# Packing the next key tile's scores into the void half of a causal diagonal block

## The chip, the cores and the metric

The kernel runs on one core of one Trainium2 chip, as one launch. The metric is the time of a run on the device in microseconds (us), lower is better. Engines are called as in the profile: PE is TensorE's matmul side, PEld its weight loads, ACT is ScalarE, DVE is VectorE, POOL is GpSimd, SP is SyncE, which issues the DMAs.

## The reference

The layer has 2048 tokens of width 576 and 32 heads of width 18, cut into 4 segments of 512 tokens. Weights and activations are bfloat16. Inside a segment attention is causal; between segments a compressive memory is read and updated. A feed-forward network of width 4608 follows.

```
for s in range(4):                         # segments of L = 512 tokens
    qs, ks, vs = q[:, :, s], k[:, :, s], v[:, :, s]        # (32 heads, 512, 18)
    p = softmax(qs @ ks.T * 18**-0.5 + causal_mask)        # exp of 512 x 512 scores for each head
    a_dot = p @ vs
    a_mem = (phi(qs) @ M) / (phi(qs) @ z + 1e-6)           # memory; phi(t) = t+1 if t>0 else exp(t)
    out_s = g * a_mem + (1 - g) * a_dot
    M += phi(ks).T @ vs;  z += phi(ks).sum(rows)
h  = x + concat(out) @ wo                  # q, k, v come from layernorm(x) @ (wq, wk, wv)
h2 = h + gelu(layernorm(h) @ w1 + b1) @ w2 + b2
```

## The kernel before

**Heads and tiles.** Four heads make a group g (8 groups). A group's transposed queries and keys lie in four bands of 32 partitions, one head in each. A score matmul takes one band: 32 rows of the array, 128 keys as weights, up to 512 queries as the moving side. Four of them, one for each band, run beside each other and write four banks of PSUM; the profile shows each as `32*128`. The value product works the other way: 128 keys are the rows, 19 columns (18 of the head and a one that sums the denominator) are the weights, four heads lie beside each other in bands of 32 columns. The profile shows it as `128*19`.

**Scores of segments 1 to 3** (`stage_A`, L1105). For 128 keys `kt` only the queries from `kt*128` on are needed, so the four key tiles of a group have 512, 384, 256 and 128 columns. Two groups (a pair) fill five steps of 512 columns by the table `STEPS` (L951), whose entries are (group of the pair, key tile, first column, width). A step is one score operation (`st`, L1163), one exp of all 4 x 512 columns on ACT (`exp`, L1167) and a mask for each diagonal block of 128 x 128 (`mask`: a product with the triangle `tri` on DVE, L1176, or a select on POOL, L1178). Half of each diagonal block is void: keys that lie behind the query. Then the group's value product (`val`, L1189) reads four such pieces, `valT` (L1197) transposes it, `rec2`, `comb` and `comb2` scale it and add the memory's part (`mem`, L1134 or L1137, `memT`, `memfin`). Per segment there are 20 steps, 8 `val` and 32 masks.

**Scores of segment 0** (`stage_A0`, L970) are made in smaller portions as soon as tokens are there: 20 steps in parts A00 to A03 (`st0`, L1002; exp L1005). Six of them hold four diagonal blocks of 128 columns each (16 matmuls); the others hold off-diagonal or wide pieces.

**The exp's results** go to five buffers `pt` of 128 x 4 x 512. A score step takes four of the eight PSUM banks.

**The rest of PE's work.** Projections (`Pk`, `Pq`, `Pv`, L835, 64 rows), the output projection (`Po`, `Ro`, L793, or L819 where both lie next to each other and are done with 128 rows), transposes (L738, L881), memory sums (`M`, L928), the network's first product (`F1`, L1301 and L1338, 64 rows) and its second (`F2`, L1388, 128 rows).

**The order** is a table written by a planner outside the kernel. `TIMETABLE` (L25) gives each operation its rank and its engine, `schedule` (L396) emits all operations by rank, and each engine then runs its own list strictly in that order. Semaphores between the engines follow from which tiles are read and written, in the order of emission. The cost figures in `add(...)` serve the planner and the choice of buffers only.

**The start.** DVE fills a part of the first `pt` buffer with zeros (`warm_ok`, L638); PE runs eight matmuls on it (`warm`, L644) until the first layernorm is there, then transposes it (`TX`, L738). POOL builds the identity matrix, the triangle, and fills padding.

Of the kernel before, what the change touches and what calls it, by code (L numbers as in the profile page):

```python
# [12 lines left out]
ALU = mybir.AluOpType  # L13
# [12 lines left out]
    "A00exp": "a 75 88",  # L26
    "A00mask": "g 93 111 177 101",
    "A00st0": "p 69 87",
    "A01comb": "d156 g187 g201 g210",
    "A01exp": "a 125 141 165 152",  # L30
    "A01mask": "g127 g126 d168 g181",
    "A01oT": "d 179 191 229 218 231",
    "A01rec": "d 153 159 195 207",
    "A01st0": "p 124 140 164 147",
    "A01swap": "d225 g230",
    "A01val": "p 150 184",
    "A01valT": "d 151 157 192 206",
    "A02comb": "g 318 352",
    "A02exp": "a 204 222 214 247 259 277 291",
    "A02mask": "g261 g242 g260 d320",  # L40
    "A02rec": "d 287 342",
    "A02st0": "p 198 221 213 237 252 270 290",
    "A02val": "p 274 278 307 324",
    "A02valT": "d 279 326",
    "A03comb": "g 416 446",
    "A03exp": "a 312 344 329 351 363 370 385",
    "A03mask": "g358 g345 g357 d392",
    "A03oT": "d 362 360 418 447 459",
    "A03rec": "d 378 432",
    "A03st0": "p 308 330 327 348 359 369 384",  # L50
    "A03swap": "g 448 453",
    "A03val": "p 367 372 421 422",
    "A03valT": "d 376 426",
    "A0flip": "s 110 84 113 118 160 175 284 298",
    "A1comb": "g535 d581 d630 g676 d708 g737 g773 d783",
    "A1comb2": "g549 g604 g634 g689 g719 d758 d779 d785",
    "A1eg": "a 393 430 520 593 584 653 617 714",
    "A1exp": "a 395 450 429 523 516 538 562 570 607 586 627 666 637 680 703 694 733 741 749 718",
    "A1flip": "s 383 424 470 509 488 606 583 678",
    "A1mask": "d456 g466 g515 g495 g474 g547 g537 g545 g620 g585 d572 d602 g645 g633 g643 d616 g661 d681 g672 g674 d705 d686 d712 g713 d744 g757 g756 g762 "  # L60
        "d755 d766 g730 g735",
    "A1mem": "p 442 513 578 649 613 722 691 745",
    "A1memT": "d 443 514 579 655 622 726 692 761",
    "A1memfin": "g499 d590 g611 g657 d659 d752 g747 d784",
    "A1oT": "d 673 732 798 809 810",
    "A1pq": "d 407 458 536 639 601 699 667 736",
    "A1rec": "d 462 565 589 656 652 740 697 770",
    "A1rec2": "d 521 573 625 660 698 725 772 782",
    "A1rg": "g 406 454 497 619 559 651 631 721",
    "A1st": "p 394 444 425 522 503 528 561 569 598 580 626 663 636 679 702 693 729 734 748 715",  # L70
    "A1swap": "g806 d793",
    "A1val": "p 518 568 623 646 695 723 763 780",
    "A1valT": "d 519 571 624 658 696 724 764 781",
    "A2comb": "g889 d921 d968 d997 g1029 g1063 g1127 g1148",
    "A2comb2": "g904 g922 g973 d1013 d1047 g1079 g1133 g1149",
    "A2eg": "a 751 727 872 924 984 939 1008 1052",
    "A2exp": "a 796 774 804 790 816 906 919 871 934 945 963 989 1001 979 1011 1028 1046 1078 1069 1092",
    "A2flip": "s 706 668 818 843 819 888 967 1037",
    "A2mask": "d805 d803 g788 d822 g849 d885 g855 d861 d923 g959 d937 g957 g892 g964 d954 g965 g981 d991 d992 g1016 d1025 d1032 g1042 d1014 d1070 d1090 "
        "g1050 g1098 g1085 g1096 g1128 g1104",  # L80
    "A2mem": "p 835 859 911 938 1019 971 1059 1101",
    "A2memT": "d 836 866 913 956 1024 975 1060 1102",
# [1467 lines left out]
```

## Time and profile before

| | |
|---|---|
| runs | 447.46, 448.99, 449.4 us; median 448.99 |
| profiled execution | span 444.7 us from the first to the last instruction; its own total is not given, so 4.3 us lie between the span and the median |
| PE | busy 431.7 us, 97% of the span, 5355 matmuls |
| ACT | busy 296.7 us, 67% |
| DVE | busy 291.2 us, 65% |
| POOL | busy 179.3 us, 40% |
| granted TensorE clock | 0.999 |

Times are from one profiled execution; shares are of its span. A busy share says how long an engine had an instruction in flight. PE's matmuls are pipelined, so one may start while the one before it is still counted as busy; what an operation takes from PE is read from the distance between starts. A row of the timeline gives start, length, engine, line, operation, the tiles it writes and reads, the active rows and columns of the array, the operand's shape and how many instructions it merges. A row of the waits gives the engine and line that waited, what ended the wait, the total in us, the number of times and the longest.

### The profile page before, as it was taken

How to read it: one execution, taken by the hardware profiler on the slowest of the kernel's cores; microseconds unless marked ns; L12 is line 12 of the kernel's file. 1: busy time of each engine (PE TensorE's matmuls, PEld its weight loads, DVE VectorE, ACT ScalarE, POOL GpSimd, SP SyncE). 2: the span in 40 equal slices, each digit the busy share in tenths (PEclk: the TensorE clock that was granted, in tenths of full speed). 3: DMA queues.
4: the chain of work that ended last, by engine and by line, in shares of the span. 5: the costliest groups of instructions: out<-in, count | busy, mean ns of one | idle time of the engine just before them, and what ended most of it. 6: DMA issues, size and time to landing. Idle time of an engine off the chain costs nothing.

```text
span 444.7 us, 12623 instructions
## 1 busy us (share of the span) xinstructions
PE 431.7 (97%) x5355; PEld 278.3 (63%) x5355; DVE 291.2 (65%) x636; ACT 296.7 (67%) x269; POOL 179.3 (40%) x312
## 2 busy tenths in 40 slices
PE   8888999998999999999999999999999999999997
PEld 5666677765676776664445766654457775446775
DVE  5889888999899988867777987837765121010011
ACT  5999999999878798686798966752684002556000
POOL 5776756457748435734236559440011000000010
PEclk9999999999999999999999999999999999999999
DMA  6779989999999945693863355805463461550030
GB/s 208 204 250 246 271 264 279 228 228 244 236 257 348 315 152 166 175 242 69 245 190 52 107 146 161 201 2 153 131 210 111 101 171 39 169 194 1 1 107 28
DMA packets 85274, 76.73 MB, mean 173 GB/s; under 512 B 62945, under 2 KB 72545, under 8 KB 85217
## 3 DMA queue, kind: packets, MB, share of 16 engines
q1 hardware_dynamic: 85072, 75.83, 63.3%
q8 instruction: 42, 0.69, 0.7%
q10 hardware_dynamic: 144, 0.09, 0.1%
q14 instruction: 16, 0.12, 0.1%
HBM read 42.08 MB, written 18.87 MB: 137 GB/s over the span
## 4 chain that ended last, share of the span: by engine, by line
PE 75%; DVE 7%; DMA 6%; ACT 6%; POOL 2%; issue 2%; SPq 1%; POOLq 0%; DVEq 0%; ACTq 0%
PE bank L1388 27%; PE bank L1301 21%; PE bank L835 9%; PE bank L1338 6%; DMA w1g<-in_B_w_dram 4%; PE bank L1163 3%; ACT hT L1355 3%; PE bank L1189 3%; PE bank L793 2%; DMA x<-in_A_x_dram 2%; ACT pt L1167 1%; PE bank L1002 1%; PE bank L819 1%; DVE ln L710 1%; POOL pt L1178 1%
## 5 line engine op out<-in xcount | busy, mean ns | idle before, releaser
L1167 ACT ACTIVATE pt<-bank 128x2048 bf16<-128x2048 f32 x60 | 112.7, 1878 | 30.4 <-PE bank L1163 25.1
L1388 PEld LDWEIGHTS <-hT 128*128 128x128 bf16 x1152 | 110.2, 98 | 34.5 <-issue 7.0
L1301 PE MATMUL bank<-xreg,w1g 64*128 64x512 bf16 x972 | 108.0, 376 | 0.2 <-DMA w1g<-in_B_w_dram 0.2
L1301 PEld LDWEIGHTS <-w1g 64*128 64x128 bf16 x972 | 46.2, 94 | 57.1 <-issue 2.3
L1388 PE MATMUL bank<-w,hT 128*128 128x288 bf16 x576 | 78.3, 286 | 0.0
L1388 PE MATMUL bank<-w_lo,hT 128*128 128x288 bf16 x576 | 78.0, 286 | 0.0
L835 PE MATMUL bank<-hT,xreg 64*128 64x288 bf16 x864 | 58.0, 283 | 1.1 <-DVE qk_pad L634 0.6
L1306 ACT ACTIVATE hT<-bank,b_col 128x512 bf16<-128x512 f32 x36 | 22.5, 689 | 46.0 <-PE bank L1301 46.0
L1178 POOL TENSOR_SCALAR_AFFINE_SELECT pt<-pt 128x512 bf16<-128x512 bf16 x58 | 42.0, 737 | 27.1 <-ACT pt L1167 26.9
L835 PEld LDWEIGHTS <-xreg 64*128 64x128 bf16 x864 | 41.6, 94 | 14.3 <-issue 5.0
L1400 DVE TENSOR_TENSOR ot<-bank,hc 128x288 bf16<-128x288 f32 x32 | 13.8, 448 | 52.2 <-PE bank L1388 51.1
L1316 DVE TENSOR_SCALAR hT<-bank,b_col 128x512 bf16<-128x512 f32 x49 | 34.9, 742 | 18.6 <-PE bank L1301 18.5
L1374 POOL TENSOR_TENSOR hc<-hc,b_bc 128x576 f32<-128x576 f32 x9 | 11.7, 1297 | 82.0 <-DMA hc<-hd 82.0
L1005 ACT ACTIVATE pt<-bank 128x2048 bf16<-128x2048 f32 x20 | 37.6, 1880 | 2.8 <-PE bank L1002 2.1
L1338 PE MATMUL bank<-xreg,w1g 64*128 64x256 bf16 x648 | 38.3, 269 | 0.6 <-DMA w1g<-in_B_w_dram 0.6
L1338 PEld LDWEIGHTS <-w1g 64*128 64x128 bf16 x648 | 31.3, 94 | 6.4 <-issue 2.7
L1374 DVE TENSOR_TENSOR hc<-hc,b_bc 128x576 f32<-128x576 f32 x7 | 5.6, 817 | 43.8 <-DMA hc<-hd 43.8
L1321 ACT ACTIVATE hT<-hT 128x8192 bf16<-128x8192 bf16 (+2 forms) x6 | 31.8, 5321 | 1.7 <-DVE hT L1316 1.6
L1314 ACT ACTIVATE hT<-bank,b_col 128x512 bf16<-128x512 f32 x23 | 15.1, 685 | 21.9 <-PE bank L1301 21.6
L1176 DVE TENSOR_TENSOR pt<-pt,tri 128x512 bf16<-128x512 bf16 x38 | 21.5, 569 | 4.7 <-ACT pt L1167 4.7
L1163 PE MATMUL bank<-qk 32*128 32x512 bf16 (+3 forms) x384 | 23.8, 300 | 0.2
L1349 DVE TENSOR_TENSOR hT<-bank,b_col 128x512 bf16<-128x512 f32 x32 | 21.0, 681 | 3.8 <-PE bank L1338 3.4
(117 smaller groups left out, 564.1 us busy)
## 6 DMA issues: line engine op xcount, KB each, us to landing
w1g<-in_B_w_dram SPq DMA_DIRECT2D x41, 576.0 KB, 5.0
qkd<-qk_pad SPq DMA_DIRECT2D x15, 512.0 KB, 3.9
hd<-h SPq DMA_DIRECT2D x16, 288.0 KB, 3.9
hc<-hd SPq DMA_DIRECT2D x16, 288.0 KB, 3.6
w_lo<-in_B_w_dram SPq DMA_DIRECT2D x3, 864.0 KB, 7.0
w<-in_B_w_dram SPq DMA_DIRECT2D x3, 864.0 KB, 11.1
xb<-in_A_x_dram SPq DMA_DIRECT2D x16, 144.0 KB, 4.2
x2d<-xn SPq DMA_DIRECT2D x14, 160.0 KB, 2.9
```

The source lines that it names most:

```text
L835: nc.tensor.matmul(out=out, lhsT=xTb.t[r, k, ts], rhs=wt[r, k, :], start=(k == 0), stop=(k == ND - 1))
L1005: ex = add(ps, {"act": 1.88}, lambda e: nc.scalar.activation(out=pt.t[:], in_=st.t[:], func=ACT.Exp, scale=scale), [sc], pt, [st], table=" ...
L1163: nc.tensor.matmul(out=st.t[:, i, off:off + n_], lhsT=qk[rows, 1, kt * P:(kt + 1) * P], rhs=qk[rows, 0, kt * P:L], start=True, stop=True, ...
L1167: ex = add(ps, {"act": 1.88}, lambda e, st=st, pt=pt: nc.scalar.activation(out=pt.t[:], in_=st.t[:], func=ACT.Exp, scale=scale), [sc], pt, ...
L1176: nc.vector.tensor_tensor(out=blk, in0=blk, in1=tri[:].unsqueeze(1).to_broadcast([P, 4, P]), op=ALU.mult)
L1178: nc.gpsimd.affine_select(out=blk, in_=blk, pattern=[[0, 4], [1, P]], compare_op=ALU.is_ge, fill=0.0, base=0, channel_multiplier=-1)
L1301: nc.tensor.matmul(out=cc[w].t[:], lhsT=w1.t[rows, k, q, :], rhs=x2T[s].t[rows, k, :], start=(k == 0), stop=(k == ND - 1))
L1306: ready_f[f + w] = [add(pf - 12, {"act": 0.68}, lambda e, f=f, w=w, cc=cc: nc.scalar.activation(out=hT[:, :, f + w, :], in_=cc[w].t[:].rea ...
L1316: nc.vector.tensor_scalar(out=dst, in0=src, scalar1=b, scalar2=None, op0=ALU.add)
L1321: ge = add(2.9, {"act": 0.42 * (f1 - f0) + 0.2}, lambda e, f0=f0, f1=f1: nc.scalar.activation(out=hT[:, :, f0:f1, :], in_=hT[:, :, f0:f1, ...
L1338: nc.tensor.matmul(out=cc[w].t[:, q * 2 * P:(q + 1) * 2 * P], lhsT=w1.t[rows, k, q, :], rhs=x2T[s].t[rows, k, ts], start=(k == 0), stop=(k ...
L1388: nc.tensor.matmul(out=c.t[:, 0:HALF], lhsT=hT[:, tl // 2, f, (tl % 2) * P:(tl % 2 + 1) * P], rhs=w2_c[ch][:, f - ch * WCH, hf * HALF:(hf ...
```

## The change

In a diagonal block of 128 keys x 128 queries the first 64 queries never see the last 64 keys. These 64 x 64 scores are computed, and masked, for nothing. The change writes something useful there: the scores of the next key tile's first 64 keys against that tile's first 64 queries. For an even key tile (0 and 2) four more matmuls of 64 weight columns by 64 moving columns write partitions 64 to 127 of those 64 columns (`tile_position=(32*i, 64)`), over the void scores. The odd key tiles (1 and 3) then need only 320 and 64 columns, so that a step of the two is 384 wide, and so is its exp. After the exp a new operation `hi` (`drop`) copies the packed block, masked, from partitions 64 to 127 of the even step's buffer to partitions 0 to 63 of a part of its own in the odd step's buffer (columns 384 to 511), whose other 64 partitions hold zeros, written once at the start (`Zmemset`). The even block's own mask (`cut`) runs after `hi`, since it clears the packed half. `val` reads each odd tile in two pieces.

In segment 0 the six steps of four diagonal blocks are packed in the same way and are 384 wide. The five buffers `pt` become three `pt` and two `po`. The eight `warm` matmuls write eight banks. All ranks in the timetable are new and some operations change engine; `st`, `st0`, `val` and the others keep their number.

```
-    pt_s = slots(5, [P, 4, 512], "pt")
+    pt_s = slots(3, [P, 4, 512], "pt")
+    po_s = slots(2, [P, 4, 512], "po")
...
-        STEPS = [[(0, 0, 0, 512)], [(0, 1, 0, 384), (0, 3, 384, 128)], [(0, 2, 0, 256), (1, 2, 256, 256)],
-                 [(1, 0, 0, 512)], [(1, 1, 0, 384), (1, 3, 384, 128)]]
+        STEPS = [[(0, 0, 0, 512)], [(0, 1, 64, 320), (0, 3, 0, 64)], [(0, 2, 0, 256), (1, 2, 256, 256)],
+                 [(1, 0, 0, 512)], [(1, 1, 64, 320), (1, 3, 0, 64)]]
...
# the score step of segments 1 to 3
-                                             rhs=qk[rows, 0, kt * P:L], start=True, stop=True, tile_position=(32 * i, 0))
+                                             rhs=qk[rows, 0, L - n_:L], start=True, stop=True, tile_position=(32 * i, 0))
+                        if kt % 2:
+                            continue
+                        nxt = slice((kt + 1) * P, (kt + 1) * P + 64)
+                        for i in range(4):
+                            rows = slice(32 * i, 32 * i + 32)
+                            nc.tensor.matmul(out=st.t[64:P, i, off:off + 64], lhsT=qk[rows, 1, nxt], rhs=qk[rows, 0, nxt], start=True, stop=True,
+                                             tile_position=(32 * i, 64))
...
+                cols = slice(0, 384 if odd else 512)
+                ex = add(ps, {"act": 1.47 if odd else 1.88}, lambda e, st=st, pt=pt, cols=cols: nc.scalar.activation(
+                    out=pt.t[:, :, cols], in_=st.t[:, :, cols], func=ACT.Exp, scale=scale), [sc], pt, [st], table="exp", name="exp")
...
# for each group, once both steps of the pair are listed (kt = 0 and 2)
+                    def below(kt, dg=dg, po=po, po_x=po_x):
+                        off, n_, pt, ex = of_pair[dg, kt]
+                        d0 = 384 + 32 * kt
+                        hi = add(ps, {"dve": 0.27, "pool": 0.40}, lambda e: drop(e, po.t[0:64, :, d0:d0 + 64], pt.t[64:P, :, off:off + 64], 1),
+                                 [ex, po_x, z_po] + later, None, [pt, po], name="hi")
+                        mk = add(ps, {"dve": 0.43, "pool": 0.64}, lambda e: cut(e, pt.t[:, :, off:off + P], 1, P), [hi], None, [pt], name="mask")
...
# val: kt, pieces (first query, first column, width)
+                        pieces = [(kt * P + 64 * (kt % 2), off, n_)] + ([(kt * P, 384 + 32 * (kt - 1), 64)] if kt % 2 else [])
...
# the score step of segment 0, where packed
+                at = {0: 0, 1: 128, 2: 256, 3: 192}
...
+                        if not packed or b % 2:
+                            continue
+                        for i in range(4):
+                            rows = slice(32 * i, 32 * i + 32)
+                            nc.tensor.matmul(out=st.t[64:P, i, o0:o0 + 64], lhsT=kk[rows, 4 * Q + b + 1, 1, k0:k0 + 64],
+                                             rhs=qq[rows, 4 * Q + b + 1, 0, p0:p0 + 64], start=True, stop=True, tile_position=(32 * i, 64))
...
# at the start
+        def zero_po(e):
+            for u in po_s.tiles + pt_s.tiles[0:2]:
+                VEC[e].memset(u[64:P, :, 384:512], 0.0)
+        z_po = add(0.2, {"dve": 0.9, "pool": 2.0}, zero_po, (), name="memset")
...
# timetable: the first four entries of "memset" are the zeros of warm (L638), mhalf, and the padding of qk_pad twice
-    "gate": "g 8",
+    "gate": "d 8",
-    "ident": "g 6",
+    "ident": "g 2",
-    "memset": "d1 d9 g25 g35 d0 a172 a7 a178 a68 g190 g200 g128",
+    "memset": "d4 d13 g0 g3 d30 a151 a166 a29 a46 g280 g338 g162",
+    "Zmemset": "g 1",
-    "tri": "g 48",
+    "tri": "g 6",
-    "warm": "p 13 18 29",
+    "warm": "p 5 15 21",
```

Counted from the two timetables: PE has 510 operations before and after, SP 219 and 219, ACT 254 and 264, DVE 539 and 552, POOL 249 and 257. Of the masks, 41 lay on DVE and 71 on POOL; now 29 and 59, and of the 54 `hi` 21 lie on DVE and 33 on POOL. Ten evictions (`copy`) go from DVE to ACT, three `hc` and seven `comb`/`comb2` from POOL to DVE. Of the 16 output projections 5 had `Po` and `Ro` next to each other, now 3.

99 lines of the change are left out of this document (68 added, 31 removed), and 571 rows, old and new, of the table TIMETABLE.

## The prediction

> **What bounds the kernel now.** I read the page's busy lines, the 40 slices and the chain first, then busy time by stretch, then the waits, then the timeline of PE alone.
>
> ```profile
> span 444.7 us, 12623 instructions
> PE 431.7 (97%) x5355; PEld 278.3 (63%) x5355; DVE 291.2 (65%) x636; ACT 296.7 (67%) x269; POOL 179.3 (40%) x312
> ...
> PE   8888999998999999999999999999999999999997
> ...
> ACT  5999999999878798686798966752684002556000
> ```
>
> PE is busy in every slice. The span is 444.7 us; the median of the runs, 449.0, is 4.3 us more, and I add my sum to 449.0 directly.
>
> ```profile
> 0.00:20.00 20.00, 16.73 (x221) 11.70 (x223) 14.38 (x38) 13.86 (x20) 11.65 (x27) 1.00 0.67 207
> 20.00:50.00 30.00, 27.27 (x541) 19.91 (x536) 27.42 (x71) 27.36 (x39) 21.72 (x35) 1.00 0.96 256
> 75.00:110.00 35.00, 33.07 (x585) 24.06 (x583) 32.86 (x75) 34.39 (x28) 21.73 (x46) 1.00 1.04 233
> 225.00:260.00 35.00, 35.00 (x381) 20.10 (x378) 28.09 (x61) 32.06 (x18) 16.00 (x28) 1.00 0.43 119
> 345.00:444.70 99.70, 96.37 (x823) 64.03 (x820) 11.48 (x24) 22.46 (x36) 1.51 (x2) 1.00 0.32 90
> ```
>
> Columns are length, then busy time of PE, PEld, DVE, ACT, POOL. PE idles 444.7 - 431.7 = 13.0 us in all: 3.3 in the first 20 us (waiting for the first tokens) and 3.3 in the last stretch, which has no attention. What a lighter ACT, or any better order, can give back lies in the other 6.4 us, most of it in 20 to 50 (2.7) and 75 to 110 (1.9, where ACT is busy 34.39 of 35).
>
> ```profile
> ACT pt L1167 <- PE bank L1163: 25.1, 33, 1.8
> ...
> PE bank L881 <- POOL tri L1423: 0.9, 1, 0.9
> ...
> PE bank L1002 <- ACT pt L1005: 0.8, 2, 0.6
> ...
> PE bank L1189 <- POOL pt L1178: 0.3, 1, 0.3
> ...
> PE bank L1189 <- DVE pt L1176: 0.2, 1, 0.2
> ```
>
> ACT's exps wait 25.1 us for PE's scores; PE waits for exps and masks about a microsecond altogether. PE is the bound, ACT is not. So the change is worth what it does to PE's own time, and that is read from distances between starts:
>
> ```profile
> 190.08 1.64 PE L1388 MATMUL bank<-w,hT 128*128 128x288 bf16 x12
> 191.56 0.90 PE L1388 MATMUL bank<-w_lo,hT 128*128 128x288 bf16 x6
> 192.39 0.40 PE L1163 MATMUL bank<-qk 32*128 32x256 bf16 x8
> 192.72 0.91 PE L1388 MATMUL bank<-w_lo,hT 128*128 128x288 bf16 x6
> ...
> 196.84 0.38 PE L1134 MATMUL bank<-e,MZ_blk 128*128 128x512 bf16 x1
> 197.15 0.72 PE L1189 MATMUL bank<-pt,v_aug 128*19 128x512 bf16 x16
> 197.81 0.39 PE L1163 MATMUL bank<-qk 32*128 32x512 bf16 x4
> 198.13 1.64 PE L1388 MATMUL bank<-w_lo,hT 128*128 128x288 bf16 x12
> ```
> ```profile
> 257.81 0.40 PE L1137 MATMUL bank<-e,MZ_blk 128*32 128x512 bf16 x4
> 258.04 0.72 PE L1189 MATMUL bank<-pt,v_aug 128*19 128x512 bf16 x16
> ```
> ```profile
> 14.87 0.40 PE L1002 MATMUL bank<-qk 32*128 32x128 bf16 x16 [0.15 <-ACT qk L630]
> 15.20 0.45 PE L738 MATMUL bank<-ident,xn 128*128 128x128 bf16 x5
> ```
>
> A column: 12 x 288 columns from 190.08 to 191.56 are 0.428 ns each. Six matmuls should then take 0.74 us; from 191.56 to 192.39 are 0.83, so 0.09 are left, at the point where the array changes from 128 rows to 32. The score step has 512 columns in its band (two sets of 256), 0.219 us, and takes 0.33: 0.11 are left at the change back. From L1134 (one matmul of 512 columns, 128 rows, 128 columns of weights) to L1189 (128 rows, bands of 32 columns) are 0.31, again 0.09 left, although **only the columns changed**. L1189 has 1280 columns per band, 0.548, and takes 0.66: 0.11. From L1137 to L1189 nothing changes (bands of 32 columns both) and 512 columns take 0.23: 0.01 left. So a change of the array's division costs 0.09 to 0.11 us, columns alone included, and no change costs nothing.
>
> **The change part by part.**
>
> *Score columns.* A pair of groups had 5 x 512 = 2560 columns per band. Now: 512+64, 320+64, 256+64+256+64, 512+64, 320+64, which is 2560 again. A packed step of segment 0 has 128+64+64 twice, 512 as before. In `val` the odd tiles are cut in two, 512+320+64+256+64+64 = 1280 as before. PE's columns neither shrink nor grow: 0 us.
>
> *More, smaller sets.* Four matmuls in four bands are a set. Scores go from 8 to 12 sets a pair (12 pairs, +48) and from 4 to 6 in six packed steps (+12); `val` goes from 4 to 6 in 24 groups (+48), and in segment 0 gains 12. That is 120 sets. Sixteen matmuls of 128 columns (L1002, 0.33) take what four of 512 take (L1163, 197.81 to 198.13, 0.32): at most 0.01 for three more sets, so 0.003 each, 0.4 us. The other end: a weight load that isn't hidden. In
>
> ```profile
> 96.29 0.69 PEld L1189 LDWEIGHTS <-v_aug 128*19 128x19 bf16 x16
> ```
>
> a load comes every 0.043 us on average; if a 64-column set, 0.027 us by its columns, were held that long, 120 x 0.016 = 1.9 us. I take 0.4, since the 16 small matmuls above are the nearest row. The Trainium skill, TensorEngine Tiling, Instruction Overhead, says that each matmul has some 60 cycles of overhead whatever its width. By that, at 2.4 GHz an estimate of 25 ns a set, it would be 3.0 us and the whole sum 2.6 higher; the two rows just compared show no such overhead at 128 columns, and no row here shows 64.
>
> *Changes of division inside a step.* This is the term that decides. A packed set has 32 rows and 64 columns of weights; its neighbours have 32 rows and 128. A step of one even tile has one change more (128, 64, out); the middle step has three more (128, 64, 128, 64, out); odd steps none. Per pair 1+0+3+1+0 = 5, in 12 pairs 60; a packed step of segment 0 has four more, six steps 24. Together 84. No row of before has bands of 64 columns, so the price is bounded: 0 (as L1137 to L1189) and 0.11. The nearest row is L1134 to L1189, where the rows stay and the columns change, and it pays 0.09; I take 0.10: **+8.4 us**. Of the changes between operations nothing is gained: 212 before and 213 after, counted from the two timetables. The Trainium skill, TensorEngine Tiling, Tiling Modes, lists 32x64 as a mode apart from 32x128 and says that changing the mode drains the array; the rows above agree for the modes that occur, and for 32x64 no run here shows it yet.
>
> *ACT.* Thirty exps (24 odd steps, six in segment 0) shrink from 2048 to 1536 elements.
>
> ```profile
> L1167 ACT ACTIVATE pt<-bank 128x2048 bf16<-128x2048 f32 x60 | 112.7, 1878 | 30.4 <-PE bank L1163 25.1 <-DVE pt L1176 1.4 <-issue 1.4
> ...
> L1123 ACT ACTIVATE e<-qk 128x512 bf16<-128x512 bf16 x24 | 14.9, 626 | 0.3 <-PE bank L1137 0.2
> ```
>
> Between 512 and 2048 elements an element costs (1878 - 626) / 1536 = 0.82 ns, so 0.42 us each, 12.5 us together. Ten evictions of about 0.4 us come to ACT. All of it lies beside PE's work; it counts only through the 6.4 us.
>
> *Masks and `hi`.* Instead of 112 masks there are 88 and 54 `hi`, half as large.
>
> ```profile
> L1176 DVE TENSOR_TENSOR pt<-pt,tri 128x512 bf16<-128x512 bf16 x38 | 21.5, 569 | 4.7 <-ACT pt L1167 4.7
> ```
> ```profile
> L1178 POOL TENSOR_SCALAR_AFFINE_SELECT pt<-pt 128x512 bf16<-128x512 bf16 x58 | 42.0, 737 | 27.1 <-ACT pt L1167 26.9
> ```
>
> A `hi` costs between half and a whole mask. DVE: 12 masks less (-6.8), 21 `hi` (6.0 to 11.9), ten evictions less. POOL: 12 less (-8.8), 33 `hi` (12.2 to 24.3). POOL is 60% idle, DVE 35%: 0 us. But `mask` now waits for `hi` on the same buffer and `hi` for both exps, so a `val` is ready some 0.4 to 0.7 us later, and behind it in PE's list stand all later matmuls. The cover is that PE's `val` waited 0.3 and 0.2 us for masks in the whole run. If it is gone, 24 x 0.1 = 2.4 us. Five buffers become three and two; a pair used five in turn anyway, so the same `val` frees the same step: 0 us.
>
> *The start.* `Zmemset` stands second on POOL, ahead of the identity, and writes into the first buffer `pt`, which DVE's zeros for `warm` write after it by rank. So `warm` waits for POOL.
>
> ```profile
> 0.79 0.20 POOL masks.py:197 MEMSET ident<- 128x128 bf16 x1 [0.29 <-POOLq L1534]
> ...
> 3.32 0.18 POOL L696 CAST mark<-x 1x1 f32<-1x1 bf16 x1 [1.96 <-DMA x<-in_A_x_dram]
> 3.45 0.83 POOL L610 MEMSET qk_pad<- 128x896 bf16 x1
> ```
> ```profile
> 1.78 3.59 PE L644 MATMUL bank<-pt 128*128 128x512 bf16 x8 [1.78 <-DVE pt L638]
> 5.16 1.17 PE L738 MATMUL bank<-ident,xn 128*128 128x128 bf16 x9
> ```
>
> POOL would start at 0.8 with the padding (0.83), then four fills of 512 elements at 0.83 x 512/896 = 0.47 each; the buffer in question is third, 3.0 us, then DVE's fill: `warm` starts near 3.4 instead of 1.78, and the transposes behind it near 6.8 instead of 5.16. DVE's `gate` and first layernorm (3.3) shift by some 0.5, and with `gate` (before: POOL, 3.32) the held loads in SP's queue. Against that the triangle and padding are done early, which PE waited 0.9 for. +1.7 - 0.9, I take +0.7; ends -0.5 and +1.7.
>
> *The rest of the new order.* Two output projections fewer are fused; 0. SP issues 219 operations as before. Of the 6.4 us I let 1.9 (30%) come back: ACT is 12 us lighter, and a PE that is slower by 2% leaves DVE and POOL earlier relative to it. Ends: 5 us back, 4 us lost.
>
> Sum: 8.4 + 0.4 + 0.7 - 1.9 = +7.6; **449.0 + 7.6 = 456.6 us**.
>
> **The rivals.** *(a) The 64-column bands don't count as a change.* For: rows and band positions stay as they are, and L1137 to L1189 shows that another tile of the same division is free. Against: L1134 to L1189. Without the 8.4: 449.0 - 0.8 = 448.2 us. *(b) Faster: the stalls in 20 to 50 and 75 to 110 close because ACT is lighter.* For: ACT is busy 34.39 of 35 us there. At 5 us recovered and no price for the bands 449.0 + 1.1 - 5.0 = 445.1 us. It decides only if what is recovered exceeds 84 times the price, plus 1.1, plus 2.2 for a difference that a measurement shows; with at most 6.4 to recover the price must be under 0.04 us, less than half of any change in the rows. *(c) More than forecast:* weight loads unhidden (+1.5 more), the start in full (+1.0), `val` late (+2.4): 461.5 us. *(d) The changes in segment 0 are covered* by PE's 2.7 idle us in 20 to 50: 2.4 less, 454.2; inside the forecast's range.
>
> **How the numbers follow.** Forecast 0.72, own range 452 to 461.5; (a) 0.13; (b) 0.10; (c) beyond 461.5 0.05. A measurement tells about 0.5%, 2.2 us, from no change. (a) is mostly within that (0.11), the rest faster; forecast and (c) are slower. Faster 0.12, same 0.11, slower 0.77. The range 449.0 to 461.5 holds the forecast and about half of (a).
>
> **What would show it.** PE's page line rises by some 6 to 9 us at the same columns; in the timeline a step of one even tile takes 0.43 to 0.46 us instead of 0.33, the middle step 0.6 to 0.7, an odd step 0.27; ACT's exps of 1536 elements take 1.46 us and ACT's busy time falls by about 8; `warm` starts near 3.4 us. The forecast is wrong if a step with packed sets takes 0.36 or less: then it is (a), and (b) if the waits of PE fell by several us as well.

## The result and the profile after

| | before | after |
|---|---|---|
| runs on the same chip, median | 448.49 us (447.46 to 449.4) | 454.38 us (453.18 to 455.19) |
| ratio after / before, 95% interval | | 1.0153 (1.0132 to 1.0173) |
| span of the profiled execution | 444.7 us | 451.4 us |
| PE busy / idle | 431.7 / 13.0 us | 440.3 / 11.1 us |

The changed kernel is slower by 1.5%, 6.9 us by the ratio (5.9 to 7.8), 5.9 us by the two medians. The forecast was +7.6. In the runs on record the time is 1.6 to 2.0 us over the span of the same execution, so the profile of before stands for a run of about 446.5 us (an estimate from these), faster than the four in the table; that of after stands for the fastest of its four, 453.18 us.

The page of after: the span, busy time by engine, and the shares of the chain that ended last.

```profile
span 451.4 us, 13648 instructions
...
PE 440.3 (98%) x5842; PEld 290.1 (64%) x5842; DVE 291.6 (65%) x649; ACT 291.0 (64%) x281; POOL 178.7 (40%) x325
...
PE 85%; DVE 5%; POOL 4%; ACT 2%; DMA 2%; issue 1%; SPq 0%; POOLq 0%; ACTq 0%; DVEq 0%
```

PE gained 8.6 us of busy time and lost 1.9 us of idle time; the span grew by the difference, 6.7 us. ACT got lighter by 5.7 us, and the kernel is slower all the same; what ACT's relief is worth is priced below (run e4).

The stretches of after that answer to those shown of before (225 to 260, where PE is full in both, is left out; length, then busy time of PE, PEld, DVE, ACT, POOL):

```profile
0.00:20.00 20.00, 16.03 (x217) 11.01 (x219) 13.53 (x37) 11.19 (x19) 12.06 (x29) 1.00 0.65 206
20.00:50.00 30.00, 28.67 (x608) 20.13 (x604) 25.91 (x67) 25.53 (x35) 22.58 (x42) 1.00 0.97 224
75.00:110.00 35.00, 33.93 (x633) 25.28 (x631) 32.35 (x75) 32.24 (x30) 22.96 (x46) 1.00 1.02 233
...
345.00:451.40 106.40, 103.21 (x880) 69.71 (x877) 14.94 (x36) 23.91 (x37) 8.35 (x12) 1.00 0.34 100
```

PE's idle time went from 3.3 to 4.0 us in the first 20 us, from 2.7 to 1.3 in 20 to 50, from 1.9 to 1.1 in 75 to 110, and from 3.3 to 3.2 in the last stretch. Outside the first and the last stretch it fell from 6.4 to about 4.0.

Where PE's 8.6 us come from is read from distances between starts, in the timeline of PE in after:

```profile
190.31 0.39 PE L1211 MATMUL bank<-qk 32*128 32x512 bf16 x4
190.63 0.22 PE L1218 MATMUL bank<-qk 32*64 32x64 bf16 x4
190.79 2.38 PE L1458 MATMUL bank<-w,hT 128*128 128x288 bf16 x18
...
193.31 0.34 PE L1211 MATMUL bank<-qk 32*128 32x320 bf16 x8
193.59 1.64 PE L1458 MATMUL bank<-w,hT 128*128 128x288 bf16 x12
...
195.38 0.29 PE L1211 MATMUL bank<-qk 32*128 32x256 bf16 x4
195.60 0.22 PE L1218 MATMUL bank<-qk 32*64 32x64 bf16 x4
195.76 0.29 PE L1211 MATMUL bank<-qk 32*128 32x256 bf16 x4
195.97 0.22 PE L1218 MATMUL bank<-qk 32*64 32x64 bf16 x4
196.13 0.91 PE L1458 MATMUL bank<-w,hT 128*128 128x288 bf16 x6
```

From 190.31 to 190.63 are 0.32 us for 512 columns, which alone take 512 x 0.428 ns = 0.219: 0.10 is the change from 128 to 64 weight columns. From 190.63 to 190.79 are 0.16 for 64 columns, 0.027: 0.13 is the change out of the 64-column bands. So a step with one even tile takes 0.48 us, the middle step (195.38 to 196.13) 0.75, the odd step (193.31 to 193.59) 0.28. All 24 steps with one even tile take 0.475 to 0.480 us, all 12 middle steps 0.742 to 0.747. The Trainium skill, TensorEngine Tiling (Array Packing), Tiling Modes, says that switching the tiling mode drains the array and lists 32x64 as a mode of its own; this trace shows a price at these places, 0.10 and 0.13 us, and not what it consists of.

Counted over the whole trace, the changes of division went from 210 to 295. The matmuls' columns, divided by the number of bands that work beside each other, stayed equal (405.6 and 405.4 us' worth at that rate).

The start of after, and two groups of its page:

```profile
3.58 3.45 PE L651 MATMUL bank<-pt 128*128 128x512 bf16 x8 [3.58 <-DVE mark L703]
6.87 0.44 PE L745 MATMUL bank<-ident,xn 128*128 128x128 bf16 x5
```
```profile
L1223 ACT ACTIVATE po<-bank 128x1536 bf16<-128x1536 f32 x24 | 34.8, 1451 | 12.9 <-PE bank L1211 10.7
...
L975 POOL TENSOR_SCALAR_AFFINE_SELECT po<-pt 64x256 bf16<-64x256 bf16 x30 | 13.3, 450 | 26.4 <-ACT pt L1223 23.2
```

`warm` starts 1.8 us later than before (1.78) and the transposes 1.7 us later (5.16). The shorter exp takes 1.451 us instead of 1.878. The waits of PE in after:

```profile
PE bank L651 <- DVE mark L703: 3.6, 1, 3.6
...
PE bank L1029 <- DMA w_lo<-qkd: 0.5, 1, 0.5
PE bank L1259 <- POOL pt L967: 0.4, 1, 0.4
```

After the start no cause reaches a microsecond; the largest not shown is 0.6, for exps. PE is the bound still, and busier than before.

### The profile page after: what moved, and what is told of

Same layout as the page of the kernel before. It is cut to its first block, busy times and chain, and to the rows that moved or that the text cites. A ratio compares the mean times of both kernels' runs of the same rounds, so it can differ in the third digit from the quotient of the medians.

```text
span 451.4 us, 13648 instructions
## 1 busy us (share of the span) xinstructions
PE 440.3 (98%) x5842; PEld 290.1 (64%) x5842; DVE 291.6 (65%) x649; ACT 291.0 (64%) x281; POOL 178.7 (40%) x325
## 4 chain that ended last, share of the span: by engine, by line
PE 85%; DVE 5%; POOL 4%; ACT 2%; DMA 2%; issue 1%; SPq 0%; POOLq 0%; ACTq 0%; DVEq 0%
PE bank L1458 30%; PE bank L1371 24%; PE bank L842 7%; PE bank L1408 7%; PE bank L1211 4%; PE bank L800 3%; PE bank L1259 3%; DMA w_lo<-qkd 2%; PE bank L1218 1%; PE bank L1029 1%; ACT pt L1039 1%; ACT pt L1223 1%; DVE xn L733 1%; PE bank L651 1%; PE bank L1079 1%
## 5 line engine op out<-in xcount | busy, mean ns | idle before, releaser
L1223 ACT ACTIVATE pt<-bank 128x2048 bf16<-128x2048 f32 x36 | 67.6, 1877 | 25.6 <-PE bank L1218 17.7
L1458 PE MATMUL bank<-w,hT 128*128 128x288 bf16 x576 | 76.6, 286 | 0.0
L1376 ACT ACTIVATE hT<-bank,b_col 128x512 bf16<-128x512 f32 x36 | 22.6, 688 | 48.1 <-PE bank L1371 47.8
L1223 ACT ACTIVATE po<-bank 128x1536 bf16<-128x1536 f32 x24 | 34.8, 1451 | 12.9 <-PE bank L1211 10.7
L1386 DVE TENSOR_SCALAR hT<-bank,b_col 128x512 bf16<-128x512 f32 x40 | 28.8, 743 | 20.8 <-PE bank L1371 18.4
L1444 POOL TENSOR_TENSOR hc<-hc,b_bc 128x576 f32<-128x576 f32 x6 | 7.6, 1274 | 79.0 <-DMA hc<-hd 79.0
L1384 ACT ACTIVATE hT<-bank,b_col 128x512 bf16<-128x512 f32 x32 | 20.7, 684 | 18.1 <-PE bank L1371 17.9
L1039 ACT ACTIVATE pt<-bank 128x2048 bf16<-128x2048 f32 (+1 forms) x16 | 29.2, 1828 | 2.6 <-PE bank L1029 2.5
L1211 PE MATMUL bank<-qk 32*128 32x512 bf16 (+3 forms) x384 | 24.6, 288 | 0.7 <-ACT pt L1223 0.6
L967 POOL TENSOR_SCALAR_AFFINE_SELECT po<-po 128x512 bf16<-128x512 bf16 (+1 forms) x27 | 20.6, 767 | 12.0 <-ACT po L1223 10.4
L967 POOL TENSOR_SCALAR_AFFINE_SELECT pt<-pt 128x512 bf16<-128x512 bf16 (+1 forms) x29 | 21.6, 750 | 8.3 <-DVE po L973 6.8
L975 POOL TENSOR_SCALAR_AFFINE_SELECT po<-pt 64x256 bf16<-64x256 bf16 x30 | 13.3, 450 | 26.4 <-ACT pt L1223 23.2
```

Of the source, the lines that this page charges most:

```text
L967: nc.gpsimd.affine_select(out=blk, in_=blk, pattern=[[0, 4], [1, w]] if n == 1 else [[0, 4], [0, n], [1, w]], compare_op=ALU.is_ge, fill=0 ...
L1039: ex = add(ps, {"act": 1.47 if packed else 1.88}, lambda e: nc.scalar.activation(out=pt.t[:, :, cols], in_=st.t[:, :, cols], func=ACT.Exp, ...
L1211: nc.tensor.matmul(out=st.t[:, i, off:off + n_], lhsT=qk[rows, 1, kt * P:(kt + 1) * P], rhs=qk[rows, 0, L - n_:L], start=True, stop=True, ...
L1223: ex = add(ps, {"act": 1.47 if odd else 1.88}, lambda e, st=st, pt=pt, cols=cols: nc.scalar.activation(out=pt.t[:, :, cols], in_=st.t[:, : ...
L1376: ready_f[f + w] = [add(pf - 12, {"act": 0.68}, lambda e, f=f, w=w, cc=cc: nc.scalar.activation(out=hT[:, :, f + w, :], in_=cc[w].t[:].rea ...
L1384: nc.scalar.activation(out=dst, in_=src, func=ACT.Identity, bias=b)
```

## The experiments

The theory: PE's added changes of division are the loss, and a microsecond of PE is a microsecond of time. Its rivals: the start, `hi` with the masks behind it, or the new order cost it, and the changes hardly matter.

Ratios are to the kernel before, on the same chip, with 95% intervals. Differences in us between a run and after are differences of ratios x 448 us; their bounds join both intervals as the root of the sum of squares.

**The price in the old kernel: b1_packed_unused.** The kernel before, in its own order, with the packed matmuls added: 60 sets that write scores nobody reads (they fall into void halves, which the mask clears).

```
# before: stage_A, behind each set of the score step; stage_A0 alike
+                        if kt % 2:
+                            continue
+                        nxt = slice((kt + 1) * P, (kt + 1) * P + 64)
+                        for i in range(4):
+                            rows = slice(32 * i, 32 * i + 32)
+                            nc.tensor.matmul(out=st.t[64:P, i, off:off + 64], lhsT=qk[rows, 1, nxt], rhs=qk[rows, 0, nxt], start=True, stop=True,
+                                             tile_position=(32 * i, 64))
```

> The kernel before, in its own order, with the 60 packed sets of 64 x 64 scores added to its score steps and not used: they land in the void half of the even diagonal blocks, which the masks clear. This is PE's part of the change alone: 84 changes of division, 60 exits from 64-column bands, 60 x 64 columns more. The trace after prices them at 84 x 0.10 + 60 x 0.03 + 60 x 64 x 0.428 ns = 11.8 us of PE time. Theory A (PE is the bound in every stretch): 447 + 10 to 12 = 457 to 459 us, 1.023 to 1.027 of before. Theory B (part of PE's added time falls where PE would have waited anyway; taking the changes out of the new order gave back only about 3 of 8): 451 to 454 us, 1.009 to 1.016.

Measured: 1.0190 (1.0156 to 1.0225), +8.5 us. The page and the timeline of PE in this run:

```profile
span 454.4 us, 13103 instructions
...
PE 442.4 (97%) x5595; PEld 286.8 (63%) x5595; DVE 291.9 (64%) x636; ACT 297.3 (65%) x269; POOL 178.2 (39%) x312
```
```profile
192.58 0.40 PE L1169 MATMUL bank<-qk 32*128 32x512 bf16 x4
192.91 0.22 PE L1176 MATMUL bank<-qk 32*64 32x64 bf16 x4
193.06 0.91 PE L1401 MATMUL bank<-w_lo,hT 128*128 128x288 bf16 x6
```

The step takes 0.48 us here too. PE's busy time rises by 10.7 us. Of that, 60 x 64 columns x 0.428 ns = 1.6 are the added columns, which after doesn't have; 9.1 are left for 84 changes (0.108 each). In time, 8.5 - 1.6 = 6.9 us (5.3 to 8.5) are left. Nothing else of the change is in this kernel, so PE's part alone makes a loss as large as that of the whole change. The ratio lies between the two expectations, and neither is met: 10.7 us of PE's busy time came out as 8.5 us.

**The price taken away from the new kernel: e1_wide_packed.** The packed sets keep their columns but use 128 columns of weights, like their neighbours, so that no change of division is left inside a step. They then overwrite the whole of those 64 columns: the scores of an even diagonal block's upper left 64 x 64 are left out.

```
-  nc.tensor.matmul(out=st.t[64:P, i, off:off + 64], lhsT=qk[rows, 1, nxt], ..., tile_position=(32 * i, 64))
+  nc.tensor.matmul(out=st.t[:, i, off:off + 64], lhsT=qk[rows, 1, (kt + 1) * P:(kt + 2) * P], ..., tile_position=(32 * i, 0))
```

> The changed kernel with each packed set issued with 128 weight columns at column 0 instead of 64 at column 64: same number and width of matmuls, but the array's division (32 rows, 128 columns) never changes inside a score step. It leaves out the upper-left 64 x 64 scores of each even diagonal block: the wide set writes the next tile's scores over them. Theory (the 84 changes of division are what costs): the trace after shows 0.10 to 0.11 us to enter 64-column bands and 0.03 more than usual to leave them, so 84 x 0.10 + 60 x 0.03 = about 10 us less than the changed kernel, 444 us, 0.990 of before. Rival (the 120 additional sets and their weight loads cost): stays at 454 us, 1.013. Rival (the new order itself is slow, division is beside the point): stays at 454 us.

Measured: 1.0083 (1.0055 to 1.0111), 3.1 us (1.6 to 4.7) less than after. The page, the three largest waits of PE behind the start, and the stretch of 20 to 50 us:

```profile
span 448.6 us, 13648 instructions
...
PE 432.8 (96%) x5842; PEld 284.8 (63%) x5842; DVE 291.9 (65%) x649; ACT 290.2 (65%) x281; POOL 178.3 (40%) x325
...
PE 75%; DVE 11%; POOL 4%; DMA 4%; SPq 3%; issue 2%; ACT 1%; DVEq 0%; POOLq 0%; ACTq 0%
```
```profile
PE bank L1259 <- DVE pt L965: 1.0, 1, 1.0
PE bank L1029 <- DMA w_lo<-qkd: 1.0, 1, 1.0
PE bank L842 <- DMA xreg<-xnd: 1.0, 3, 0.5
```
```profile
20.00:50.00 30.00, 26.73 (x610) 19.30 (x608) 26.64 (x67) 25.54 (x35) 22.49 (x43) 1.00 1.01 223
```

PE's busy time falls by 7.5 us, but its idle time rises from 11.1 to 15.8. In 20 to 50 us PE idles 3.3 us instead of 1.3, and the chain runs less through PE (75% instead of 85%) and more through DVE, DMA and SP's queue. The waits that appear are for a mask (0 to 1.0 on this row) and for loads (`w_lo<-qkd` 0.5 to 1.0, `xreg<-xnd` 1.0). DVE and POOL have the same work as in after (291.9 and 178.3 us against 291.6 and 178.7); I read the rows as PE arriving earlier at masks and loads that come no earlier. No expectation was met: neither the theory (0.990) nor the rivals that saw no gain at all (1.013). So the changes are part of the loss, but in the new order a microsecond off PE is worth 0.4 us of time (3.1 / 7.5; 0.2 to 0.6). The span of e1 is still 3.9 us longer than that of before, though its columns are those of before (405.4 us' worth) and its changes nearly so (211 against 210): neither of the two makes up the rest.

**Half of the changes: e2_packed_last.** In each step all sets of 128 columns come first and the packed ones last; 42 changes of the 84 go.

```
                     for (dg, kt, off, n_) in step:
                         ... # the sets of 128 columns
+                    for (dg, kt, off, n_) in step:
+                        qk = qks[2 * gp + dg].t
                         if kt % 2:
                             continue
                         ... # the packed sets
```

> The changed kernel with the sets of each score step in another order: all sets of 128 weight columns first, the packed sets of 64 last. Same matmuls. Changes of division inside the steps fall from 84 to 42 (middle steps 3 to 1, packed steps of segment 0 4 to 1). Theory: 42 x 0.11 = 4.6 us less than the changed kernel, 450 us, 1.003 of before. Rivals (sets, or the order of operations): no change, 454 us, 1.013.

Measured: 1.0143 (1.0101 to 1.0185).

```profile
PE 437.0 (97%) x5842; PEld 286.7 (63%) x5842; DVE 292.0 (65%) x649; ACT 290.7 (64%) x281; POOL 178.8 (40%) x325
```

In a span of 452.1 us PE has 3.3 us less to do than in after and idles 15.1 instead of 11.1. Of the gain nothing is to be seen beyond the interval. A miss for "a microsecond of PE is a microsecond of time".

**No change inside a step, all scores computed: e3_narrow_bands.** The even and packed steps use bands of 64 weight columns throughout: the lower 64 keys in one half of the array's columns, the packed block and the upper 64 keys in the other.

```
-  # 128 keys x n_ columns, then the packed 64 x 64
+  for (w, c0, c1, ks, qs) in ((0, 0, n_, k0, q0), (64, 0, 64, k1, k1), (64, 64, n_, k0 + 64, q0 + 64)):
+      for i in range(4):
+          nc.tensor.matmul(out=st.t[w:w + 64, i, off + c0:off + c1], lhsT=qk[rows, 1, ks:ks + 64],
+                           rhs=qk[rows, 0, qs:qs + c1 - c0], ..., tile_position=(32 * i, w))
```

> The changed kernel with every matmul of the even and packed score steps in bands of 64 weight columns: the lower 64 keys against all queries, beside it in the other column half first the packed block and then the upper 64 keys against the queries they need. No change of division inside a step, and the packed block lies beside the lower keys' columns instead of behind them: per pair 2560 columns become 2304, per packed step 512 become 384, together 3840 columns x 0.428 ns = 1.6 us less. Theory: 454.4 - 10 - 1.6 + (36 + 6 steps that now all leave from 64-column bands, already in the 0.03) = 443 us, 0.987 of before. Rival (the two column halves of a row band don't run beside each other, or loads of 64 weight columns are slow): each such step 0.15 to 0.2 us longer than in theory, 449 to 452 us, 1.00 to 1.01.

Measured: 1.0093 (1.0057 to 1.0129), 2.7 us (0.8 to 4.5) less than after. The page, the timeline of PE, and a timeline row and the stretch of 44 to 48 us:

```profile
PE 434.8 (96%) x6130; PEld 287.8 (64%) x6130; DVE 291.2 (65%) x649; ACT 290.5 (64%) x281; POOL 178.1 (40%) x325
```
```profile
192.93 0.43 PE L1223 MATMUL bank<-qk 32*64 32x512 bf16 x12
193.29 2.38 PE L1463 MATMUL bank<-w,hT 128*128 128x288 bf16 x18
...
197.89 0.43 PE L1223 MATMUL bank<-qk 32*64 32x256 bf16 x24
198.25 0.91 PE L1463 MATMUL bank<-w,hT 128*128 128x288 bf16 x6
```
```profile
43.80 3.77 PE L842 MATMUL bank<-hT,xreg 64*128 64x288 bf16 x36 [1.77 <-DMA xreg<-xnd]
```
```profile
44.00:48.00 4.00, 3.91 (x44) 2.02 (x40) 1.45 (x3) 0.72 (x3) 1.31 (x3) 0.64 1.08 411
```

Both kinds of step take 0.36 us, where after takes 0.48 and 0.75: the two column halves run beside each other, and what is saved is the changes and 64 columns for each packed block. The ratio falls into the rival's range, but not for the rival's reason, which these rows exclude: what PE gave back came out as waits. PE's busy time falls by 5.5 us; in a span of 450.8 its idle time rises to 16.0. One of its waits, 1.77 us for the load `xreg<-xnd`, is followed by a granted clock of 0.64 over 4 us (half from 45.1 to 48.6 us), and 36 matmuls took 3.77 us; the same count takes 2.38 us in the run e8 below. PE's busy time in e3 holds these 1.4 us, lost at one place. They belong to the profiled execution (mean clock 0.996, 452.56 us); the three other runs of e3 had 1.0 and took 450.1 to 451.92 us.

**That wait moved: e8_narrow_flip_first.** e3, with one load of SP (`A0flip`, the eighth) ranked behind the two loads it stood ahead of.

```
-    "A0flip": "s 88 79 112 113 173 174 274 198",
+    "A0flip": "s 88 79 112 113 173 174 274 200.5",
```

> The changed kernel with even and packed score steps in bands of 64 columns throughout (as e3_narrow_bands, 1.009 of before), and in SP's list the last transposing load of segment 0's keys (needed late) behind, instead of ahead of, the two transposing loads of segment 1's first tokens. In the trace of the narrow bands PE waits 1.8 us at 43.8 for that load, and the 36 matmuls after it take 3.77 us instead of 2.38. Theory (once PE's price of division is gone, the new order's transposing loads on SP are what holds PE): 2.5 to 3.7 us less than with the narrow bands alone, 1.001 to 1.004 of before. Rival (the stall only moves on to the next wait): 1.006 to 1.010.

Measured: 1.0063 (1.0044 to 1.0081), 4.0 us (2.8 to 5.3) less than after. The page, the same place of PE's timeline, and waits of PE:

```profile
PE 433.1 (96%) x6129; PEld 286.7 (64%) x6130; DVE 291.2 (65%) x649; ACT 290.5 (65%) x281; POOL 179.0 (40%) x325
```
```profile
42.55 2.38 PE L842 MATMUL bank<-hT,xreg 64*128 64x288 bf16 x36
```
```profile
PE bank L826 <- ACT qk_pad L637: 1.1, 1, 1.1
PE bank L842 <- issue: 1.1, 1, 1.1
```

The wait and the slowed clock are gone, and PE's busy time with them (1.7 less than e3), but in a span of 449.0 us the idle time stays at 15.9: PE waits 1.1 us for ACT and 1.1 us on issue instead. The theory (1.001 to 1.004) is missed; the rival, that the stall moves on to the next wait, holds. Against e3 the time is 1.3 us less (-0.5 to +3.2), not clear of zero. This is the best version of the change found, and it is still 0.6% slower than the kernel before, with PE at nearly the same busy time (433.1 against 431.7).

**ACT's relief given back: e4_exp_as_before.** The exp of the first 64 columns of each shortened step is done twice, 30 more ACT instructions; nothing else is changed.

```
-  nc.scalar.activation(out=pt.t[:, :, cols], in_=st.t[:, :, cols], ...)
+  for part in ((slice(0, 64), cols) if odd else (cols,)):
+      nc.scalar.activation(out=pt.t[:, :, part], in_=st.t[:, :, part], ...)
```

> The changed kernel with ACT's saving taken back: after each of the 30 exps of 384 columns the exp of their first 64 columns is done once more, 256 elements x 0.82 ns plus about 0.2 us of fixed cost, 0.4 us each, 12 to 13 us of ACT altogether. Theory (PE is the bound, ACT's relief is worth little): 454.5 to 456 us, 1.013 to 1.017 of before. Rival (ACT's relief gave back what the 3 us of closed stalls in the trace after show, and more): 458 us or over, 1.022; if ACT were the bound, 467 us.

Measured: 1.0238 (1.0206 to 1.0270), 3.8 us (2.1 to 5.5) more than after.

```profile
PE 442.3 (97%) x5842; PEld 290.2 (64%) x5842; DVE 290.7 (64%) x649; ACT 301.3 (66%) x311; POOL 178.6 (39%) x325
```

ACT is 10.3 us busier, and in a span of 456.0 us PE idles 13.7 instead of 11.1 (busy 2.0 more). The theory, that ACT's relief is worth little, is missed, and the rival holds: the shorter exps are worth some 4 us in this order, although ACT is busy only 64 to 66% of the span.

**The late start put into the old kernel: b2_late_start.** Before, with POOL filling four tiles (that DVE's zeros for `warm` wait for) ahead of the identity, and `gate` on DVE.

```
-    "gate": "g 8",
+    "gate": "d 3.5",
...
-    "memset": "d1 d9 g25 g35 ...",
+    "Zmemset": "g -1",
+    "memset": "d1 d9 g-2 g35 ...",
...
+        def zero_po(e):
+            for u in pt_s.tiles[3:5] + pt_s.tiles[0:2]:
+                VEC[e].memset(u[64:P, :, 384:512], 0.0)
```

> The kernel before, in its own order, with the start of the change: POOL first fills one padding buffer and then four stretches of 64 x 512 elements, one of them in the buffer that the zeros for the first eight matmuls are written to, and the gate of the held loads runs on DVE. The first matmul starts near 3.6 us instead of 1.8, the first transposes near 6.9 instead of 5.2. Theory (the late start reaches the end, as the new order's runs without changes of division suggest, which stay 3 to 4 us above before): +1 to +1.8 us, 1.002 to 1.004. Rival (it is absorbed by the waits in 13 to 50 us): within 0.5 us, 1.000.

Measured: 1.0010 (0.9993 to 1.0027).

```profile
3.59 3.60 PE L645 MATMUL bank<-pt 128*128 128x512 bf16 x8 [3.59 <-DVE mark L697]
6.97 1.27 PE L739 MATMUL bank<-ident,xn 128*128 128x128 bf16 x10
```

The start is as late as in after (3.58, 6.87), and the time shows 0.4 us (-0.3 to +1.2): the rival, that the waits after it absorb it, fits better than the theory's 1 to 1.8 us.

**The early start put into the new kernel: e5_warm_third, and into e3: e6_narrow_warm_third.** The zeros for `warm` go into a buffer that POOL doesn't fill.

```
-    warm = pt_s.tiles[0][:, 0, :]
+    warm = pt_s.tiles[2][:, 0, :]
```

> The changed kernel with the zeros of the first eight matmuls in the third buffer, which the fills for the packed blocks do not touch, so that DVE and PE do not wait for POOL: first matmul near 1.8 us, first transposes near 5.2 us. Theory (late start reaches the end): 1 to 1.8 us less than the changed kernel, 1.011 to 1.013 of before. Rival (absorbed): as the changed kernel, 1.015.

> The changed kernel with even and packed score steps in bands of 64 columns throughout, and the zeros of the first matmuls in the third buffer. Theory (the price of division and the late start add): the narrow bands alone gave 1.009 of before with a stall of 1.8 us and a slowed clock after it at 44 us in their trace; with the earlier start 1.000 to 1.006. Rival (what is taken from PE turns into other waits): 1.007 to 1.011.

Measured: e5 1.0140 (1.0104 to 1.0176), e6 1.0123 (1.0074 to 1.0173). The start of e5:

```profile
5.41 0.71 PE L745 MATMUL bank<-ident,xn 128*128 128x128 bf16 x5 [0.57 <-DVE xn L731]
```

The transposes start 1.5 us earlier than in after, and the time doesn't follow: e5 stands 0.6 us (-1.3 to +2.4) below after, between the theory and the rival, and e6 can't be told from e3 (1.0093); its ratio lies above both ranges named for it, its interval reaches into the rival's. Three of its four runs had a mean granted clock of 0.992 to 0.996, and they are the slower ones (451.98 to 454.94 us, against 451.65 at 0.999). No loss of more than e5's interval lies in the start.

**`hi` made small: e7_hi_small.** The 48 `hi` of segments 1 to 3 copy 8 columns; the packed blocks' other columns are left out of the value product (they count as zero).

```
-  drop(e, po.t[0:64, :, d0:d0 + 64], pt.t[64:P, :, off:off + 64], 1)
+  drop(e, po.t[0:64, :, d0:d0 + 8], pt.t[64:P, :, off:off + 8], 1, 8)
...
-  VEC[e].memset(u[64:P, :, 384:512], 0.0)
+  VEC[e].memset(u[:, :, 384:512], 0.0)
```

> The changed kernel with the 48 hi of segments 1 to 3 on 8 columns instead of 64 (32 elements for 256); the packed blocks' other columns are left out of the product and count as zero. Takes about 48 x 0.25 us from DVE and POOL and shortens the chain exp, hi, mask, val by the same. Theory (hi lies beside PE's work): as the changed kernel, 1.012 to 1.016 of before. Rival (the longer chain to val holds PE in the new order): 2 us or more less, under 1.010.

Measured: 1.0134 (1.0104 to 1.0163). The group of these copies on POOL:

```profile
L975 POOL TENSOR_SCALAR_AFFINE_SELECT po<-pt 64x32 bf16<-64x32 bf16 x30 | 8.7, 295 | 27.6 <-ACT pt L1223 24.4 <-PE bank L1371 1.9
```

POOL's `hi` is 0.155 us shorter, a third, and the time 0.9 us (-0.8 to +2.5) less: nothing that can be told from zero, as the theory had it. It excludes a large cost of the copy's length; a cost of its mere presence, the extra link from exp to mask, isn't tried by it.

**The change in the old order: f2_old_order and f1_old_order_narrow.** The whole change with the ranks of before; `hi` stands just ahead of its mask, some of the ranks of segments 0, 1 and 3 are moved by hand where the new dependences ask for it, and the zeros for `warm` lie in the third buffer. f2 has after's score sets, f1 those of e3.

```
-    (after's TIMETABLE)
+    (before's TIMETABLE, with "A1hi": "g455.98 g494.98 ...", "Zmemset": "g6.5", and moved: A02val, A02st0, A02exp, A03val, A03st0, A03exp, A1st, A1exp, A3exp)
```

> The whole change (packed sets with 64-column bands, exps of 384 columns, hi, three and two buffers) in the order of the kernel before: its ranks and engines, with hi put just before the mask that follows it, and 9 of 510 PE ranks and 7 exp ranks moved a little because the buffers now are of two kinds; the zeros of the first matmuls lie in the third buffer, the fills stand behind the identity. It differs from the run with unused packed sets (1.019 of before) by the shorter exps and by hi, masks and buffers. Theory (PE's part costs 9, ACT's relief gives back about 4, the new order is neutral): 1.009 to 1.015 of before, as the changed kernel. Rival (the new order itself is worse than the old one, as the run without changes of division suggests, which stays 0.8% above before): 1.003 to 1.007. Rival (hi and the two kinds of buffers cost as much as ACT gives): 1.019 or more.

> As f2_old_order, and even and packed score steps in bands of 64 columns throughout, so that no step changes the array's division inside and 3840 columns (1.6 us) fall away. Theory (old order, PE bound): PE's part is then -1.6 us instead of +9, ACT's relief up to -4: 0.988 to 0.997 of before, faster than both. Rival (hi, masks and buffers hold the val back): 1.000 to 1.006. Rival (what PE does not spend becomes other waits, as in the new order): 0.997 to 1.003.

Measured: f2 1.0555 (1.0525 to 1.0585), f1 1.0360 (1.0320 to 1.0401). The page of f2 with its largest wait of PE, and the page of f1:

```profile
PE 447.0 (95%) x5831; PEld 292.5 (62%) x5832; DVE 293.0 (62%) x643; ACT 285.4 (61%) x269; POOL 186.1 (39%) x339
```
```profile
PE bank L1204 <- ACT pt L1216: 3.6, 3, 1.7
```
```profile
PE 437.7 (94%) x6119; PEld 288.9 (62%) x6120; DVE 293.7 (63%) x643; ACT 285.0 (61%) x269; POOL 186.1 (40%) x339
```

The spans are 471.6 and 463.9 us, of which PE idles 24.6 and 26.2: the hand-moved order opens waits of its own, 3.6 us of them for exps alone. Both traces also hold two stretches of 3.4 us at half the granted clock (mean 0.992; from 33.8 and 136.2 us in f2, from 39.9 and 135.5 in f1), up to 3.4 us lost in each run. None of the expectations held, and what the new order costs or gains against the old one can't be read from these two. What can be read is their difference, since they share the order: 1.95% (1.45 to 2.45), 8.7 us, for 9.3 us less of PE's busy time.

## Why the prediction came out

The time, +5.9 to +7.8 us by the ratio, holds the forecast's +7.6 near its upper end. The term that was to decide, the changes of division, is there and priced. That the total fits so well is partly luck: the changes cost more than forecast, and less waiting made up for it.

*Columns, 0.* Right: 394.5 and 394.8 us' worth.

*More, smaller sets, +0.4.* Too small to be measured by itself. An odd step, two sets without a change between them, takes 0.28: 384 columns are 0.164, the usual change out 0.11, which leaves no room for the larger end.

*Changes of division, +8.4.* Right in count (85 more against 84), a fifth too low in price. Going into a 64-column band costs about the forecast's 0.10 (median of 60: 0.108), coming out 0.13 (0.127), where 0.11 is usual, so the steps lie above the ranges named for them (0.48 against 0.43 to 0.46, 0.75 against 0.6 to 0.7). Summed over the steps this is 12 x (2 x 0.12 + 0.37) = 7.3 us for the pairs and, with 0.81 instead of 0.33 us in six packed steps of segment 0, 2.9 more, 10.2 together. The page's PE rose by 8.6: besides the columns and the changes, each kind of change at its usual price in the traces (0.09 to 0.13), PE's busy time holds 4.8 us in before and 3.4 in after. I take most of the difference for short waits that the counted end of the matmul before covers; no run shows it by itself. Rival (a) is out: the step takes 0.48, not 0.36 or less. Rival (b) is out with it.

*"So the change is worth what it does to PE's own time."* This nearly holds in the old order (b1: PE +10.7, time +8.5; f1, with the ranks moved by hand, against f2: PE -9.3, time -8.7). It does not hold for taking the work out of the new order: e1 gave back 3.1 us for 7.5 of PE, e2 nothing measurable for 3.3, e8 4.0 for 7.2. The waits that PE's added work had covered came out, for masks and for loads in SP's queue. No run plans a new order for the cheaper steps, so whether e3's bands would then beat the kernel before stays open. So the forecast's sum was right as a sum, but its reading, that the 84 changes are the whole cause, is only partly borne out. With the changes gone (e1, e8) the kernel is still 0.6 to 0.8% slower than before, although ACT is lighter. If prices from different orders may be added, which no run shows, PE's part (+6.9, b1) and ACT's relief (-3.8, e4) leave 3.8 us of the measured +6.9 to something else. Which part of the remainder is the new order, the two kinds of buffers, or `hi` as a link between exp and mask, stays open: f1 and f2 were to tell, and brought waits of their own.

*ACT.* The exp's 1.451 us was forecast (1.46). ACT's busy time fell by 5.7 us, not 8: the evictions that came to it were taken at 4 us, and 30 x 0.427 - 5.7 = 7.1 came back. What a lighter ACT is worth was mis-sized the other way. The forecast let 1.9 us come back for all of ACT's relief and the order together; e4, which gives back 10.3 us of ACT's busy time, prices the relief alone at 3.8 (2.1 to 5.5).

*The rest of the new order, -1.9.* PE's idle time outside the first and the last stretch fell by 2.4, near the 1.9 let in. But e1 shows that this wasn't a gift of the order: without the changes the idle time is 15.8 us, above the 13.0 of before.

*Masks and `hi`, 0.* The durations lie between half and a whole mask, as bounded (0.450 on POOL against 0.737, 0.355 on DVE against 0.569). PE's largest wait for a mask is 0.4 us, so the cover named (0.3 and 0.2 us of waiting) nearly held. e7 finds no cost beyond its interval.

*The start, +0.7.* `warm` at 3.58 (forecast 3.4) and the transposes at 6.87 (6.8). PE's idle time in the first 20 us rose by 0.7, as taken. In time b2 and e5 agree with 0.7 and with 0.

*Rival (d)*, 454.2 us, in which PE's idle time in 20 to 50 us covers segment 0's changes, lies nearest to the median of 454.38, but it is added to 449.0, while before has 448.49 beside after: as a difference it is +5.2, outside the +5.9 to +7.8, and the forecast's +7.6 is inside. That stretch's idle time did fall from 2.7 to 1.3 us, and rose to 3.3 in e1. It speaks for a part of (d), no more.

## What to carry to other kernels

When small matmuls are packed into free room, count the changes of the array's division they bring, columns too: at 0.10 to 0.13 us each they cost more here than the saved exps gave. Where a packed block is narrower than its neighbours, make the neighbours as narrow and let both halves run beside each other, as e3 does, rather than switch within a step; here that made the step cheap (0.36 us) and the kernel still 0.6 to 0.9% slower than without packing. And price PE's work in the order that the engines will run: at 97 to 98% busy a microsecond of PE was worth 0.8 to 0.9 us in the old order and 0.4 (0.2 to 0.6) in the new one, where waits lay just beneath it. An engine at 64% can count as well: 10 us of ACT cost 3.8.

## What the runs showed of the hardware that I had not expected

Leaving a 64-column band takes 0.13 us, entering it 0.10. Two column halves of the same row bands run beside each other: in e3 twelve matmuls, each half with 512 columns for every band, take 0.36 us from start to start, against 0.33 for four of 512 at full width in the kernel before. And a single wait of 1.77 us in e3 was followed by half the granted clock from 45.1 to 48.6 us (1.4 us lost on 36 matmuls, which took 2.38 us in e8, where that wait is gone). In the 3.4 us just before, PE was busy 1.55 us. The four stretches at half clock in f1 and f2 are as long, and PE was busy 1.4 to 1.8 us in the 3.4 us before each. That alone doesn't bring it about: in the profile of e6 PE was busy only 1.0 us from 41.8 to 45.2, and the clock stayed full. What decides, no run tells.
